# Zero fills, filler products, block means and token buffers in the lead-in of an attention kernel

## The chip, the core and the metric

The kernel runs on one core of a Trainium2 chip. The metric is device time in microseconds (us) of one execution, as the median over runs. The time before the change is 1376.94 us, the median of 3 runs (1375.19 to 1377.54).

## The reference

Three stages follow each other in float32: a sparse attention, a soft mixture of experts over its output, and a two-layer network with a rational activation. Only the attention is touched. It has 2 batches, 8 heads, 768 tokens and head dimension 64. Each query sees the keys less than 16 positions away, and besides them one summary per block of 32 keys: the maximum of the keys, and the mean of the values.

```python
k_sum = k.reshape(B, H, nb, block, D).max(axis=3)
v_sum = v.reshape(B, H, nb, block, D).mean(axis=3)
scores_l = scale * np.matmul(q, k.transpose(0, 1, 3, 2))
mask_l = np.abs(pos[:, None] - pos[None, :]) < window
scores_s = scale * np.einsum('bhsd,bhnd->bhsn', q, k_sum) + np.log(block)
scores_all = np.concatenate([np.where(mask_l, scores_l, -1e9), scores_s], axis=-1)
a = exp(scores_all - max) ; a = a / (sum(a) + 1e-09)
out = np.matmul(a, np.concatenate([v, v_sum], axis=2))
```

Its output, 1536 tokens by 512, is the input of the mixture (8 experts with all tokens in all of them, and a balancing of the gates by rows and columns) and then of the last network.

## The kernel before, in words

Each engine executes its instructions in the order in which the program writes them; a wait on another engine stops all that stands behind it on the same engine. The order is thus the order of the Python code, with one helper: `at(s, f, ...)` puts a function on a list (`todo`) that is worked off near the end of step `s`.

Tokens of k and q are handled in groups of 256 (`LT`), three per batch. A group is loaded by one DMA from the sync engine (`load_nat`, L345) into a buffer of the pool `nat`, copied into token order (`by_token`, L411 and the copy helper L333), transposed on TensorE in two halves of four transposes (`transpose8`, L357) and evacuated from PSUM, by ScalarE in the lead-in (`place`, L366). Which buffer of the pool a new load takes is decided when the program is built; with three buffers the first load of v has to take one that a group of k has occupied.

For the block keys, VectorE takes maxima over the transposed k (`block_keys`, L378, for groups 0 and 1; `last_keys`, L390 and L393, for group 2, straight from PSUM). The evacuation of group 1 is ordered behind the maxima over group 0, because both touch the same tile `kb`.

For the block means of v, GpSimd adds pairs of tokens (`sum_v`, L436), TensorE multiplies with an averaging matrix (`prep_v`, L446, three products of 512 columns that count as six instructions), ScalarE copies the result from PSUM (L453), and GpSimd copies it into the value buffers `vx` of the first three tiles (`block_values`, L333).

Queries are then worked off in 24 tiles of 64 tokens. Step `s` of the main loop (L735) issues, for several tiles at different stages: the scores of tile `s` (`scores`, L517, then the mask addition L524 and the row maximum L528 on VectorE), the outputs of tile `s - 3` (`av`, L567), the transposes of tile `s - 2`'s probabilities (`trans`, L550, evacuated at L552), in the first six steps five filler products on the identity matrix (`spin(5)`, L429), the normalisation of tile `s - 1` on VectorE (`norm`, L541 to L544), the exponentials of tile `s` on ScalarE (`exps`, L537), and the `todo` list of the step. A float32 product on TensorE counts as two MATMUL and two LDWEIGHTS instructions; a transpose counts as one of each.

Ahead of all this stands the setup. GpSimd makes the identity matrix and the masks (`make_mask`, L586 to L594), VectorE spreads the mask over the partitions (L599) and fills `ones`, `wavg`, `am`, the edges of `kb` and `vx` with constants (L611 to L629). `am` are the three probability buffers of the tiles, 128x544 each; `vx` are the three value buffers, 120x512 each.

After the attention, the mixture and the last network run on TensorE for more than 1200 us. Some of their first products and weight loads are mixed into the attention's steps (`main`, `dma_w`).

Of the kernel before, what the change touches and what calls it, by code (L numbers as in the profile page):

```python
# [10 lines left out]
F32 = mybir.dt.float32  # L11
F32R = mybir.dt.float32r
# [10 lines left out]
def kernel(  # L23
# [14 lines left out]
    nc = tc.nc  # L38
    B, H, S, D = q.shape
    NT, DM = out.shape  # L40
    NE, _, FE = w1.shape
    F2 = w_out.shape[0]
    P = 128
# [14 lines left out]
    NB = S // BLK  # L58
    HQ = QT // 2
    VO = 2 * HQ  # L60
    CK = VO + NB
    CO = CK + HQ
# [248 lines left out]
    with ExitStack() as actx:  # L311
        apool = actx.enter_context(tc.tile_pool(name="att", bufs=2, side="right"))
        a1 = actx.enter_context(tc.tile_pool(name="att1", bufs=1, side="right"))
# [3 lines left out]
        am = [a1.tile([P, 2 * AS], F32, name=f"am{i}") for i in range(3)]  # L317
        vx = [a1.tile([CO, DM], F32, name=f"vx{i}") for i in range(3)]
        qs = [a1.tile([P, NP, LT], F32, name=f"qs{i}") for i in range(2)]
        wavg = a1.tile([P, 2 * NB], F32, name="wavg")  # L320
        wavgr = a1.tile([P, 2 * NB], F32R, name="wavgr")
        masks = [a1.tile([P, 4 * HQ + 2 * NB + 2 * (CO - HQ)], F32, name=f"mask{i}") for i in range(3)]

        nat = {}
        kT = {}
# [6 lines left out]
        def pcopy(dst, src):  # L332
            nc.gpsimd.tensor_scalar(out=dst, in0=src, scalar1=1.0, scalar2=0.0, op0=ALU.mult, op1=ALU.add)  # L333

        def load_nat(src, nm, b, i):

            if nm == "q" and b == 0 and i < 2:
                if i:
                    t = spool.tile([P, KC, 2 * P], F32, tag="stg", name="q_0_1")
                else:  # L340
                    t = kb[1].rearrange("p c n -> p (c n)")[:, 0:NP * LT].rearrange("p (c n) -> p c n", c=NP)
                t = t.rearrange("p c (h t d) -> p (c h) t d", h=2, t=2)
            else:
                t = apool.tile([P, H, 2, D], F32, tag="nat", name=f"{nm}_{b}_{i}", bufs=3)
            nc.sync.dma_start(t, src[b, :, i * LT:(i + 1) * LT, :].rearrange("h (p t) d -> p h t d", t=2))  # L345
            nat[nm, b, i] = t

# [71 lines left out]
        def prep_q(b, i):  # L419
            new_q(b, i)  # L420
            for par in range(2):
                place(qT[b, i], par, transpose8("q", b, i, par), qscale, (b, i) == (0, 2))

        def spin(n):

            ps = psm.tile([P, 512], F32, tag="mm", name=f"spin_{len(spins)}")
            spins.append(n)
            for i in range(n):
                nc.tensor.matmul(ps[:, 0:P], lhsT=ident, rhs=ident, start=True, stop=True)  # L429
# [9 lines left out]
        def prep_v(b, *parts):  # L439
            if parts[0] == 0:  # L440
                vps[b] = psm.tile([P, DM], F32, tag="mm", name=f"vps_{b}")
            ps = vps[b]
            nb = LT // BLK
            for i in parts:
                o = (NB - nb) - nb * i
                nc.tensor.matmul(  # L446
                    ps[VO:CK, :], lhsT=wavg[:, o:o + NB],
                    rhs=nat.pop(("vsum", b, i)).rearrange("p h d -> p (h d)"),
                    start=(i == 0), stop=(i == NL - 1), tile_position=(0, VO),
                )  # L450
            if parts[-1] == NL - 1:
                vs[b] = acc[3 + 4 * b]
                (nc.vector.tensor_copy if b else nc.scalar.copy)(vs[b][VO:CK, :], ps[VO:CK, :])  # L453

        def means_split(i):
            x = nat.pop(("vsum", 1, i)).rearrange("p h d -> p (h d)")
            if i < 2:
                y = spool.tile([P, KC, 2 * P], F32R, tag="stg", name=f"vhl_{i}").rearrange("p (a b) f -> p a (b f)", a=2)
            else:
                y = apool.tile([P, 2, DM], F32R, tag="nat", name="vhl_2", bufs=3)  # L460
            nc.scalar.copy(y[:, 0], x)
            nc.gpsimd.tensor_sub(y[:, 1], x, y[:, 0].bitcast(F32))
            means[i] = (y[:, 0], y[:, 1])
# [94 lines left out]
        def av(t):  # L558
            aT = st.pop((t, "aT"))
            if t < 4 and t % 2:  # L560
                ps = psm.tile([P, NP * P], F32, tag="mm", name=f"xo_{t}").rearrange("p (c n) -> p c n", c=NP)
            else:
                ps = psa.tile([P, NP, P], F32, tag="xo", name=f"xo_{t}")
            aT = aT.rearrange("p (s j c q) -> p s j c q", s=2, j=2, c=NP)
            for p in range(NP):
                for j in range(2):
                    nc.tensor.matmul(  # L567
                        ps[j * D:(j + 1) * D, p, 0:QT],
                        lhsT=vx[t % 3][:, (2 * p + j) * D:(2 * p + j + 1) * D],
                        rhs=aT[:, :, j, p, :],  # L570
                        start=True, stop=True,
                    )
            o = t * QT
            dh, dl = xh[:, :, o:o + QT], xl[:, :, o:o + QT]
            nc.scalar.copy(dh, ps[:, :, 0:QT])
            nc.vector.tensor_sub(dl, ps[:, :, 0:QT], dh.bitcast(F32))
# [7 lines left out]
        def make_mask():  # L584
            m = masks[1]
            nc.gpsimd.memset(m, 0.0)  # L586
            nc.gpsimd.memset(m[:, VO:VO + 2 * (HQ + NB)].rearrange("p (s n) -> p s n", s=2)[:, :, 0:NB], math.log(BLK))
            lo = m[:, 0:2 * CK].rearrange("p (s n) -> p s n", s=2)[0:HQ, :, 0:HQ]
            hi = m[:, HQ:HQ + 2 * (CK + NB)].rearrange("p (s n) -> p s n", s=2)[0:HQ, :, 0:HQ]
            nc.gpsimd.affine_select(  # L590
                out=lo, in_=lo, compare_op=ALU.is_ge, fill=NEG, base=-1,
                pattern=[[0, 2], [1, HQ]], channel_multiplier=-1,
            )
            nc.gpsimd.affine_select(  # L594
                out=hi, in_=hi, compare_op=ALU.is_ge, fill=NEG, base=-1,
                pattern=[[0, 2], [-1, HQ]], channel_multiplier=1,
            )
            for p in range(1, NP):
                nc.vector.tensor_copy(m[p * HQ:(p + 1) * HQ, 0:2 * CK], m[0:HQ, 0:2 * CK])  # L599

        def edge_mask(i):
            m = masks[i]
            pcopy(m[:, 0:2 * CK], masks[1][:, 0:2 * CK])
            if i == 0:
                nc.gpsimd.memset(m[:, 0:WIN], NEG)
            else:
                nc.gpsimd.memset(m[:, 2 * CK - WIN:2 * CK], NEG)

        make_mask()
        edge_mask(0)  # L610
        nc.vector.memset(ones, 1.0)  # L611
        nc.vector.memset(wavg, 0.0)
        for m in (wavg[:, NB - LT // BLK:NB],):
# [6 lines left out]
                out=m, in_=m, compare_op=ALU.is_ge, fill=0.0, base=BLK // 2 - 1,  # L620
                pattern=[[BLK // 2, LT // BLK]], channel_multiplier=-1,
            )
        for t_ in am:
            nc.vector.memset(t_, 0.0)
        nc.vector.memset(kb[0][:, :, 0:WIN], 0.0)
        nc.vector.memset(kb[0][:, :, S + WIN:S + 2 * WIN], 0.0)
        nc.scalar.copy(wavgr, wavg)
        for t_ in vx:
            nc.vector.memset(t_, 0.0)  # L629

        def place_k(i, early=False):
            new_k(0, i)
# [36 lines left out]
        def at(s, f, *args):  # L669
            todo.setdefault(s, []).append(lambda: f(*args))  # L670
# [3 lines left out]
        at(9, edge_mask, 2)  # L674
        for o in (0, S + WIN):
            at(2, nc.vector.memset, kb[1][:, :, o:o + WIN], 0.0)
        at(2, block_values, 0)
        at(2, load_nat, k, "k", 1, 1)
        at(2, dma_w, 0, 2, 0, 6)
# [48 lines left out]
        def main(s, us):  # L728
            if mains and mains[0][0] <= s:
                credit[0] += us  # L730
            while mains and mains[0][0] <= s and credit[0] >= mains[0][1] / 2:
                credit[0] -= mains[0][1]
                mains.pop(0)[2]()

        for s in range(NQ + AV):  # L735
            if s < NQ:
                scores(s)
            if s == 2:
                prep_v(0, 0, 1, 2)
            if s == 3:  # L740
                prep_q(0, 1)
            if s >= AV:
                av(s - AV)
                if s - AV + 3 < NQ:
                    load_vx(s - AV + 3)
            main(s, 1.5 if s < 12 else 0.9 if s < 22 else 0)
            if 0 <= s - AV + 1 < NQ:
                trans(s - AV + 1)
                if s < 6:
                    spin(5)  # L750
            if 0 < s <= NQ:
                norm(s - 1)
            if s < NQ:
                exps(s)
                if s == 1:
                    sum_v(0, 2)
                if s == 1:
                    by_token("q", 0, 1)
            for f in todo.pop(s, []):
                f()  # L760
            if s < 22:
                main(s, 0.8 if s < 12 else 0.4)
            elif s < NQ + AV - 1:
                mains.pop(0)[2]()
# [544 lines left out]
```

## Time and profile before

| | |
|---|---|
| median of 3 runs | 1376.94 us (1375.19 to 1377.54) |
| the profiled execution | 1377.25 us, of which the span is 1375.5 us |
| PE (TensorE matmul) busy | 1353.9 us, 98% |
| DVE (VectorE) busy | 1063.6 us, 77% |
| ACT (ScalarE) busy | 516.3 us, 38% |
| POOL (GpSimd) busy | 796.7 us, 58% |
| mean granted TensorE clock | 0.996 of full speed |

The profile is that of one execution, and its times count from the first instruction. PEld is the weight load of TensorE, SP the sync engine, which issues the DMAs. A chain of waits is followed back from the last instruction, at each step to what released it; "issue" in it is time in which the engine waited for nothing that the profile shows. L517 is line 517 of the kernel.

### The profile page before, as it was taken

The page shows a single profiled execution, that of the slowest core. Times are in us where ns is not written, and L with a number is a line of the kernel's source. Part 1 is how long each engine was busy: PE and PEld are TensorE (multiplying, and loading weights), DVE is VectorE, ACT ScalarE, POOL GpSimd, SP SyncE. Part 2 cuts the span into 40 slices and gives each one's busy share as a digit, 9 for nine tenths or more (in the row PEclk, how much of TensorE's full clock was granted, in tenths as well). Part 3 has the DMA queues.
Part 4 walks back from the last instruction along what each step waited for, and adds up shares of the span by engine and source line. Part 5 has one row for each costly group of instructions (what it writes and reads, how often), then busy time and mean ns, then how long its engine had stood idle before and what let it go on. Part 6 is the DMA issues. An engine that isn't in the chain of part 4 may idle for free.

```text
span 1375.5 us, 22596 instructions
## 1 busy us (share of the span) xinstructions
PE 1353.9 (98%) x8547; PEld 1199.1 (87%) x8547; DVE 1063.6 (77%) x1844; ACT 516.3 (38%) x1156; POOL 796.7 (58%) x955
## 2 busy tenths in 40 slices
PE   6999999999999999999999999999999999999998
PEld 4888898899889998899988998899988888888887
DVE  5875578777777877777777777777777689998885
ACT  4676422322222222222222222222222369966662
POOL 3543546777777777677777777677777012222221
PEclk8999999999999999999999999999999999999999
DMA  9541012222222222222222222222221421212102
GB/s 235 140 112 24 16 47 66 67 75 67 82 79 78 76 71 71 67 68 72 75 71 90 74 69 66 76 66 75 68 81 59 139 75 47 77 46 92 31 16 77
DMA packets 119277, 102.55 MB, mean 75 GB/s; under 512 B 30464, under 2 KB 100224, under 8 KB 119168
## 3 DMA queue, kind: packets, MB, share of 16 engines
q1 hardware_dynamic: 119168, 101.10, 24.5%
q8 instruction: 68, 1.11, 0.4%
q14 instruction: 41, 0.34, 0.1%
HBM read 81.15 MB, written 19.92 MB: 73 GB/s over the span
## 4 chain that ended last, share of the span: by engine, by line
PE 95%; DVE 2%; ACT 2%; issue 1%; DMA 0%; POOL 0%; ACTq 0%; POOLq 0%; DVEq 0%
PE p_v L186 12%; PE p_v L187 12%; PE p_v L188 12%; PE p L186 8%; PE p L188 8%; PE p L187 7%; PE X L1092 6%; PE X L1094 6%; PE X L1093 6%; PE Z L1094 3%; PE Z L1093 3%; PE Z L1092 3%; PE Y L1094 2%; PE Y L1093 2%; PE Y L1092 2%; PE sc L517 1%
## 5 line engine op out<-in xcount | busy, mean ns | idle before, releaser
L1204 DVE SCALAR_TENSOR_TENSOR accs<-p_v,Pt,accs 128x512 f32<-128x512 f32 x336 | 244.3, 746 | 90.9 <-PE p_v L188 90.4
L186 PE MATMUL p_v<-w2h_v,hh_v 128*128 128x512 f32 x720 | 282.6, 392 | 0.0
L188 PE MATMUL p_v<-w2h_v,hl_v 128*128 128x512 f32 x720 | 281.7, 391 | 0.0
L187 PE MATMUL p_v<-w2l_v,hh_v 128*128 128x512 f32 x720 | 281.4, 391 | 0.0
L1101 DVE SCALAR_TENSOR_TENSOR hl_v<-s,hh_v 128x384 fp32r<-128x384 f32 x180 | 133.8, 743 | 76.2 <-ACT hh_v L1100 75.0
L236 POOL TENSOR_TENSOR hl<-ta,hh 128x512 fp32r<-128x512 f32 (+1 forms) x52 | 63.1, 1214 | 206.4 <-ACT hh L235 163.5
L1112 ACT COPY s<-X 128x384 f32<-128x384 f32 x56 | 27.1, 484 | 411.2 <-PE X L1094 411.2
L902 POOL TENSOR_SCALAR ce<-ce 128x296 uint32<-128x296 uint32 (+1 forms) x56 | 67.2, 1200 | 181.3 <-DVE ce L893 181.3
L186 PEld LDWEIGHTS p_v<-w2h_v,hh_v 128*128 128x128 f32 x720 | 135.2, 188 | 29.4 <-issue 3.1
L188 PEld LDWEIGHTS p_v<-w2h_v,hl_v 128*128 128x128 f32 x720 | 135.1, 188 | 28.7
L187 PEld LDWEIGHTS p_v<-w2l_v,hh_v 128*128 128x128 f32 x720 | 135.2, 188 | 25.6
L1100 ACT ACTIVATE hh_v<-s 128x384 fp32r<-128x384 f32 x180 | 95.0, 528 | 124.3 <-DVE s L1135 66.7
L112 POOL TENSOR_TENSOR wS<-S,wS 128x256 fp32r<-128x256 f32 x120 | 100.1, 834 | 14.4 <-ACT wS L109 4.7
L186 PE MATMUL p<-xh,w1h 128*128 128x512 f32 (+2 forms) x288 | 103.0, 358 | 0.0
L187 PE MATMUL p<-xl,w1h 128*128 128x512 f32 (+2 forms) x288 | 101.7, 353 | 0.5 <-issue 0.5
L188 PE MATMUL p<-xh,w1l 128*128 128x512 f32 (+2 forms) x288 | 101.8, 353 | 0.0
L186 PE MATMUL p<-w2h,hh 128*128 128x512 f32 (+1 forms) x244 | 95.0, 389 | 0.5 <-DVE accs L264 0.5
L188 PE MATMUL p<-w2h,hl 128*128 128x512 f32 (+1 forms) x244 | 94.5, 387 | 0.2 <-POOL hl L236 0.2
L187 PE MATMUL p<-w2l,hh 128*128 128x512 f32 (+1 forms) x244 | 94.3, 386 | 0.0
L112 POOL TENSOR_TENSOR w2l_v<-sb,w2h_v 128x512 fp32r<-128x512 f32 x60 | 82.8, 1380 | 5.0
L1094 PE MATMUL X<-th,wS 128*128 128x384 f32 x240 | 80.2, 334 | 0.0
L1093 PE MATMUL X<-tl,wS 128*128 128x384 f32 x240 | 80.2, 334 | 0.0
(225 smaller groups left out, 3352.1 us busy)
## 6 DMA issues: line engine op xcount, KB each, us to landing
sa<-in_moe_w_dram SPq DMA_DIRECT2D x30, 512.0 KB, 3.5
sb<-in_moe_w_dram SPq DMA_DIRECT2D x30, 512.0 KB, 4.1
cv<-in_moe_w_in_dram SPq DMA_DIRECT2D x24, 296.0 KB, 2.9
w1h<-f_in SPq DMA_DIRECT2D x16, 256.0 KB, 2.9
w1l<-f_in SPq DMA_DIRECT2D x16, 256.0 KB, 3.3
w2h<-f_out SPq DMA_DIRECT2D x16, 256.0 KB, 4.8
w2l<-f_out SPq DMA_DIRECT2D x16, 256.0 KB, 5.1
f_in<-ch SPq DMA_DIRECT2D x24, 148.0 KB, 4.2
```

The lines of the kernel that those rows point to most:

```text
L112: nc.gpsimd.tensor_sub(lo, src, hi.bitcast(F32))
L186: nc.tensor.matmul(ps, lhsT=sh, rhs=mh, start=(i == 0), stop=False)
L187: nc.tensor.matmul(ps, lhsT=sh, rhs=ml, start=False, stop=False)
L188: nc.tensor.matmul(ps, lhsT=sl, rhs=mh, start=False, stop=(i == n_k - 1))
L236: nc.gpsimd.tensor_sub(hl[:, :n], ta, hh[:, :n].bitcast(F32))
L902: nc.gpsimd.tensor_scalar(out=e, in0=e, scalar1=896, scalar2=0, op0=ALU.subtract, op1=ALU.max)
L1092: nc.tensor.matmul(ps, lhsT=w[:, 0, t], rhs=mh, start=start and t == 0, stop=False, **go)
L1093: nc.tensor.matmul(ps, lhsT=w[:, 0, t], rhs=ml, start=False, stop=False, **go)
L1094: nc.tensor.matmul(ps, lhsT=w[:, 1, t], rhs=mh, start=False, stop=t == 1, **go)
L1100: nc.scalar.activation(hh, src, AF.Relu)
L1101: nc.vector.scalar_tensor_tensor(out=hl, in0=src, scalar=0.0, in1=hh.bitcast(F32), op0=ALU.max, op1=ALU.subtract)
L1204: nc.vector.scalar_tensor_tensor(out=a, in0=ps, scalar=Pt[:, g, e:e + 1], in1=a, op0=ALU.mult, op1=ALU.add)
```

## The change

The `am` fills go to GpSimd and stand behind the rest of the setup. The spreading of the mask becomes a function of its own that VectorE executes behind the `vx` fills, and the copy of the mask for the first tile (`edge_mask(0)`) stands behind it. Ten filler products are issued ahead of the first transposes. The block means of v are no longer issued straight after the scores of step 2 but from that step's `todo` list, which is worked off behind the transposes of tile 0, five filler products and the exponentials of tile 2. The pool of token buffers has four instead of three; two of the three mask tiles are made smaller.

```diff
-        masks = [a1.tile([P, 4 * HQ + 2 * NB + 2 * (CO - HQ)], F32, name=f"mask{i}") for i in range(3)]
+        masks = [a1.tile([P, 4 * HQ + 2 * NB + 2 * (CO - HQ) * (i == 1)], F32, name=f"mask{i}") for i in range(3)]
...
-                t = apool.tile([P, H, 2, D], F32, tag="nat", name=f"{nm}_{b}_{i}", bufs=3)
+                t = apool.tile([P, H, 2, D], F32, tag="nat", name=f"{nm}_{b}_{i}", bufs=4)
...
-                y = apool.tile([P, 2, DM], F32R, tag="nat", name="vhl_2", bufs=3)
+                y = apool.tile([P, 2, DM], F32R, tag="nat", name="vhl_2", bufs=4)
...
+
+        def spread_mask():
+            m = masks[1]
             for p in range(1, NP):
                 nc.vector.tensor_copy(m[p * HQ:(p + 1) * HQ, 0:2 * CK], m[0:HQ, 0:2 * CK])
...
         make_mask()
-        edge_mask(0)
         nc.vector.memset(ones, 1.0)
         nc.vector.memset(wavg, 0.0)
...
-        for t_ in am:
+        spin(10)
+        for t_ in vx:
             nc.vector.memset(t_, 0.0)
         nc.vector.memset(kb[0][:, :, 0:WIN], 0.0)
         nc.vector.memset(kb[0][:, :, S + WIN:S + 2 * WIN], 0.0)
+        spread_mask()
         nc.scalar.copy(wavgr, wavg)
-        for t_ in vx:
-            nc.vector.memset(t_, 0.0)
+        edge_mask(0)
+        for t_ in am:
+            nc.gpsimd.memset(t_, 0.0)
...
+        at(2, prep_v, 0, 0, 1, 2)
         at(2, block_values, 0)
...
             if s < NQ:
                 scores(s)
-            if s == 2:
-                prep_v(0, 0, 1, 2)
             if s == 3:
                 prep_q(0, 1)
```

## Rows read from the trace of the kernel before

**Rows 1.** The page's chain that ended last, share of the span by engine
```profile
PE 95%; DVE 2%; ACT 2%; issue 1%; DMA 0%; POOL 0%; ACTq 0%; POOLq 0%; DVEq 0%
```
**Rows 2.** Chain in order of time up to 16 us: start, length, engine, tile, line
```profile
3.46 0.51 DVE am L624
...
6.41 0.48 DVE vx L629
6.89 0.29 DVE accs L411
...
7.32 1.95 PE kps L357 x8
...
9.29 0.65 ACT kb L366
...
9.96 1.23 DVE ks L378
...
11.28 1.15 ACT kb L366 x2
...
14.90 0.90 DVE ks L393
```
**Rows 3.** The same chain, from 15.8 to 47 us
```profile
15.84 0.64 PE sc L517 x37
...
17.16 1.04 PE sc L517 x41
...
19.80 2.29 issue
...
22.41 5.24 PE vps L446 x6
27.65 0.58 PE at L550 x4
28.23 1.12 PE spin L429 x10
29.35 0.73 PE sc L517 x46
30.08 1.02 PE qps L357 x8
...
46.30 0.45 issue
```
**Rows 4.** Windows: length, busy (count) PE, PEld, DVE, ACT, POOL; PEclk, DMA, GB/s
```profile
17.00:18.00 1.00, 0.84 (x64) 0.84 (x64) 0.62 (x2) 0.31 (x2) 0.67 (x1) 0.63 1.17 290
...
27.00:28.00 1.00, 1.00 (x5) 0.42 (x5) 0.00 (x0) 0.32 (x1) 0.00 (x0) 0.75 1.08 356
```
**Rows 5.** Tile k, first 15 us: its loads (duration ns, first to last start), landing
```profile
L345 SPq DMA_DIRECT2D k<-in_k_dram x3: 432/567/1309, 0.8 to 1.9; - x3
...
DMA to landing us min/median/max: 5.5/6.1/6.7
```
**Rows 6.** Timeline by engine: start, length, operation, shapes [idle before, releaser]
```profile
1.32 0.39 POOL L586 MEMSET mask<- 128x352 f32 x1
...
8.68 1.20 POOL L333 TENSOR_SCALAR accs<-k 128x512 f32<-128x512 f32 x2 [4.33 <-DMA k<-in_k_dram]
10.39 0.62 POOL L333 TENSOR_SCALAR accs<-kb 128x512 f32<-128x512 f32 x1 [0.51 <-DMA kb<-in_q_dram]
...
5.00 0.62 ACT L411 COPY accs<-k 128x512 f32<-128x512 f32 x1
...
20.69 0.53 DVE L544 TENSOR_TENSOR am<-am,sm 128x352 f32<-128x352 f32 x1
```
**Rows 7.** DMA queues, 19 to 20 us: packets, MB, share of 16 engines
```profile
q8 instruction: 1, 0.02, 7.2%
```
**Rows 8.** Sync engine, 9 to 12 us: what it waited for, and its issue
```profile
SPq L345 <- POOL accs L333: 1.3, 1, 1.3
...
9.91 0.37 SPq L345 DMA_DIRECT2D v<-in_v_dram  x1
```

## The prediction

> **What bounds the kernel now.** I read the page's chain of waits first. It lies on TensorE for 95% of the span [rows 1], so the long middle can't gain from this change, whose edits end at about 30 us, and every microsecond won there before TensorE becomes continuously busy should reach the end. So I next read the chain in order of time over the first 48 us, where the reader is to see two stretches that are not matmul work at full speed.
>
> The first runs up to the first scores [rows 2]. VectorE's fills of `am` and `vx` end at 6.89 us; the first copy of k follows them at once; TensorE starts at 7.32; then ScalarE and VectorE alternate (evacuate, reduce, evacuate, reduce) until the block keys are ready and the scores against them start at 15.84. The second [rows 3] is scores of tiles 0 to 2, an "issue" wait of 2.29 us in the middle of tile 2's scores, the block means of v (5.24 us for six products), tile 0's transposes and ten filler products, until tile 3's scores start at 29.35. From there TensorE shows almost no idle time up to 42 us.
>
> Then the windows by microsecond, for the clock [rows 4]: TensorE goes from 2.4 to 1.2 GHz within 17 to 18 us and back within 27 to 28 us, so the block means run at 1.2 GHz.
>
> **Fills to GpSimd, and the order of the rest on VectorE.** The three `am` fills (0.51 us each with 0.06 between, 1.7 in all [rows 2]) leave VectorE, and three mask copies move behind the `vx` fills. VectorE no longer waits for GpSimd's mask before its fills, so it is through them near 3.1 us instead of 6.89. What is late next is the data. The three k transfers are issued from 0.8 to 1.9 us and the known ones land after 5.5 and 6.7 us [rows 5]: the second at about 6.8, the third at 8.6, where GpSimd's wait for it ends [rows 6]. At that spacing of 1.8 us the first lands at 5.0 (estimate); ScalarE's copy of it at 5.00, right behind the preceding instruction, says not later [rows 6]. So the first VectorE copy moves from 6.89 to about 5.05: 1.84 us. On GpSimd the fills cost about 0.6 each by its 128x352 fill (0.39 [rows 6], scaled by columns), 1.8 us between about 3.6 and 5.4; its next work waits for data until 8.68 [rows 6], which hides them. Without that cover they would delay the third k tile by their 1.8 us.
>
> **Ten products ahead of the data.** They are twenty instructions. Ten take 1.12 us at 2.4 GHz [rows 3], so twenty take 2.2 us, or 4.5 us at 1.2 GHz, from about 1.45 (the identity is written before GpSimd's mask fill of 1.32 [rows 6]) to 3.7 or 5.95. TensorE is idle there today. What they buy is the clock for the first transposes: eight of k take 1.95 us from 7.32 [rows 2], eight of q 1.02 us from 30.08 [rows 3]. The windows' column prints 1.00 at 7.32 as well as at 30.08, but the pace is half.
>
> [...] By the printed 1.00 the products would buy nothing, and the first link would gain the 1.84 us alone.
>
> From both sides: if the clock stays at 1.2 GHz until the fillers end at 5.95 and beyond, the eight transposes end at 5.95 + 1.95 = 7.9 instead of 9.27, a gain of 1.4. If it is up by 5.5 (5.05 plus the 0.43 from copy to TensorE), they take about 1.0, and the next limit is the second k tile: landed at 6.8, two copies of 0.36 on VectorE ahead of the reduce there, which then starts at 7.55 instead of 9.96, a gain of 2.4. I take 2.0, since the clock may rise anywhere in between. The links behind keep their lengths (reduce 1.23, two evacuations 1.15, reduces and maximum [rows 2]), and the others are in time: the third k tile is copied by 9.9, and q lands at about 10.35 [rows 6], is copied, transposed and evacuated by about 13. So the scores against block keys start at 13.8 instead of 15.84.
>
> **The wait of 2.29 us, and forty more instructions.** The filler adds 20 products and 20 weight loads ahead of everything. The wait is for no engine; a 16 KB packet of the instruction queue moves in 19 to 20 us [rows 7], and work resumes at 22.09. I read it as TensorE waiting for its next block of instructions. Its end stands 6.25 us behind the start of the block-key scores, in which I suppose the request falls. Forty instructions earlier in the stream the stop comes some 20 products sooner; those are then left over behind it, 0.5 us at the pace of 41 in 1.04 [rows 3]. The request also comes sooner, by nothing up to 0.8 us (the stretch from the q evacuation to the block keys, 13.0 to 13.8). I take 0.5. The two cancel: tile 2's scores end 2.0 us earlier, at 20.4.
>
> [...]
>
> **Block means behind tile 0's transposes.** Six products (5.24), four transposes (0.58) and ten fillers (1.12) [rows 3] change places; TensorE is in order and works off the same 6.94 us. All are in the stretch in which the clock rises, 5.1 us after its start; which of them comes first doesn't change how much is done before and after that. From both sides: a rise some 1.7 us later or earlier costs or gives half of that, 0.85. I take nothing. Tile 2's exponentials no longer stand behind the means' copy on ScalarE; but TensorE had no wait for them, so nothing is won there. What is new: tile 0's outputs need the means through a ScalarE copy and a GpSimd copy, 0.6 each [rows 6] with about 0.25 of signalling, and TensorE covers that with tile 3's scores and the q transposes, 0.73 + 1.02 [rows 3]. That leaves 0.3 of cover; without it the cost would be at most 1.45. Tile 0's normalised rows, which the transposes now ahead of the means wait for, end today at 21.22 [rows 6], and 2.0 earlier at 19.2, in time for 20.4.
>
> **A fourth token buffer.** Today the first v load waits for the third k tile's copies (1.3 us of that at the end) and is issued at 9.91 [rows 8]. With a free buffer it is issued behind q at about 5, and v, q and the weights land some 2 us earlier. No step of the chain up to 31 us waits for them, so I take nothing; the bounds are a loss of 0.2 (q's last packets) and nothing gained.
>
> **Sum.** 2.0 + 0 + 0 = 2.0, and 0.1 for the 0.45 us wait of the same kind at 46.30 [rows 3], which sits elsewhere after the change and may go (ends: all of it gained, or a loss of 0.3). The profiled execution took 1377.25 (span 1375.5 and 1.75 around it); 1375.15 would follow. It lies 0.3 above the median of 1376.94, to which the same 2.1 applies: 1374.8. The forecast's own range, with 1.4 to 2.4 for the first link and 0.85 either way for the clock, is 1373.3 to 1376.2.
>
> **Rivals.** *The block of instructions comes in time.* For it: the stop may fall where the request has long been out. Against: scores eat instructions as fast as before. Then TensorE would be through tile 2's scores by 17.7, and tile 0's normalisation is late next: transposes at 19.2 instead of 22.41, a gain of 3.2, 1373.7. *The clock holds, or is back before the means.* For it: more work ahead of the scores. Against: scores of three tiles and the wait are as thin as today, when the clock fell there. The means would take half of 5.24, a gain of 2.1 + 2.6 = 4.7, 1372.2. *The clock falls early.* TensorE's work between 8 and 13 us now comes in pieces that transfers pace; if the clock falls there, the q transposes (1.0 more) and two tiles' scores (0.4 each) slow down: 2.1 - 1.8 = 0.3, 1376.6. *Slower: the instruction stream becomes the bound.* Between 29 and 46 us TensorE runs short instructions back to back, and the 0.45 at 46.30 shows the stream close to its limit. If the shifted blocks stop it twice more for 2.29, the loss is 4.6 - 2.1 = 2.5, 1379.4; one such stop already eats the gain, and slower than before begins at 2.1 us of new stops. Against it: blocks that TensorE reaches earlier are also requested earlier.
>
> **How the numbers follow.** Forecast 0.50, instructions in time 0.11, clock held 0.12, clock early 0.17, stream-bound 0.10. About 0.2% (2.75 us) is what a measurement here can tell from no change. Above that gain lie some 0.3 of the forecast's chance, most of the first rival's and all of the second's: 0.35. Slower by more than that is under half of the last, with the runs' own spread of 2.35 us added: 0.07. The rest, 0.58, is within. The range 1371.9 to 1377.2 leaves out the stream-bound case and half of the held clock.
>
> **What would show it.** First VectorE copy of k at 5.05; eight first transposes in 1.0 to 1.95 us, ended by 7.9; scores against block keys near 13.8; an "issue" wait of about 2 us inside tile 2's scores, with more products behind it; the means after the fillers; tile 3's scores near 27.3 with no wait of tile 0's outputs behind; v issued near 5. Wrong would be: the first copy still behind fills, the q transposes at half pace, or several new "issue" waits between 27 and 46 us.

## The result and the profile after

The changed kernel takes 1388.04 us (median of 4 runs, 1385.92 to 1389.65) against 1376.70 for the kernel before (median of 4 runs): a ratio of 1.0083 with a 95% interval of 1.0065 to 1.0100. It is 11.3 us slower; the forecast was 1374.8. The profiled execution took 1389.65, with a span of 1387.9 against 1375.5. The page's chain that ended last, share of the span by engine, hardly differs from [rows 1]:

```profile
PE 93%; DVE 2%; ACT 1%; issue 1%; DMA 1%; POOL 1%; SPq 0%; ACTq 0%; DVEq 0%; POOLq 0%
```

The start did what was forecast. The timeline of VectorE, GpSimd and TensorE in the first 14 us of the changed kernel (start, length, engine, line, operation, tiles, count, idle before and its end):

```profile
5.06 0.45 DVE L411 COPY accs<-k 128x512 f32<-128x512 f32 x1 [1.40 <-DMA k<-in_k_dram]
...
4.19 1.81 POOL L634 MEMSET am<- 128x544 f32 x3
...
1.42 4.39 PE L429 MATMUL spin<-ident 128*128 128x128 f32 x20 [1.42 <-POOL ident masks.py:199]
5.65 1.04 PE L357 MATMUL kps<-ident,accs 128*128 128x128 f32 x8
...
13.08 0.35 PE L517 MATMUL sc<-kb,qs 64*32 64x64 f32 x16 [0.33 <-ACT qs L366]
13.21 0.27 PE L517 MATMUL sc<-ks,qs 64*32 64x24 f32 x16
```

The copy of k starts at 5.06 instead of 6.89, the first transposes end at 6.7 instead of 9.27 [rows 2]. The scores against the keys of the tokens (`kb`) start at 13.08, those against the block keys (`ks`) at 13.21 instead of 15.84. The chain of waits from 16.9 to 29 us (start, length, what):

```profile
16.91 3.25 issue
...
20.70 1.04 PE at L550 x4
21.74 2.13 PE spin L429 x10
23.87 3.71 PE vps L446 x6
...
28.32 1.02 PE qps L357 x8
```

It answers to [rows 3]: the q transposes that stood at 30.08 now stand at 28.32, 1.76 us earlier, although the wait in front has grown from 2.29 to 3.25. Up to here the change is a gain.

The loss comes later. In the table of TensorE's waits in the first 150 us (line, waited for, total, times, longest), the kernel before has for "issue" only the two waits of [rows 3], 2.29 in scores and 0.45 in a product of the next stage. The changed kernel has:

```profile
PE xo L567 <- issue: 8.1, 3, 3.7
PE sc L517 <- issue: 3.2, 1, 3.2
```

The 8.1 us are new: three waits inside the output products of a tile (`xo`), at which no engine is waited for. The chain of the changed kernel shows where each lies and what follows:

```profile
43.12 1.10 issue
...
51.01 3.35 issue
54.36 0.48 PE xo L567 x3
...
55.36 0.21 PE p L187
...
94.52 0.65 PE xo L567 x15
95.17 3.66 issue
98.83 0.27 PE xo L567
...
99.82 0.43 PE p L187
```

The products `p` of the next stage behind the second and the third wait take 0.21 and 0.43 us each. In the chain of the kernel before, the first-layer products take 0.12 each, and the second-layer ones 0.23:

```profile
52.50 0.12 PE p L187
...
90.65 0.43 PE p L186
91.08 0.23 PE p L187
```

The windows of the changed kernel tell why (length, busy share and count of PE, PEld, DVE, ACT, POOL; then the granted clock, DMA share, GB/s):

```profile
53.00:54.00 1.00, 0.00 (x0) 0.00 (x0) 0.00 (x0) 0.00 (x0) 0.40 (x1) 0.60 0.03 8
54.00:55.00 1.00, 0.64 (x4) 0.52 (x4) 0.00 (x0) 0.12 (x1) 0.00 (x0) 0.50 0.00 0
...
60.00:61.00 1.00, 1.00 (x69) 0.78 (x67) 0.64 (x1) 1.00 (x5) 0.00 (x0) 0.98 0.23 28
...
98.00:99.00 1.00, 0.17 (x1) 0.00 (x0) 0.00 (x0) 0.00 (x0) 1.00 (x2) 0.50 0.08 14
104.00:105.00 1.00, 1.00 (x18) 0.62 (x24) 0.00 (x0) 0.45 (x1) 0.00 (x0) 0.80 0.00 0
```

TensorE stood idle from 51.01 and from 95.17 us, the granted clock fell from 1.00 to 0.50 while it was idle (the window from 53 us prints 0.60, that from 98 us 0.50), and the twelve products behind each wait were run at 0.50 before it rose again near 60 and 104 us (0.98 and 0.80 in the windows from there).

The account goes by the starts of the output products of each tile in both traces. Tiles 0 to 4 stand 1.8 us earlier than before. The wait of 1.10 in tile 4 takes the place of the one of 0.45 at 46.30 [rows 3], 0.7 lost. Between the starts of tile 5's and tile 6's outputs 5.7 us are lost: the wait of 3.35, and 2.4 by which the work behind it takes longer at the granted clock of 0.50. At tile 14's it is 6.25: 3.66, and 2.5 at 0.50 (twelve products in 5.4 instead of 3.0 us). -1.8 + 0.7 + 5.7 + 6.25 = +10.85 at tile 15, which holds through tile 23. Most of the rest of the 12.4 us between the two spans comes near 711 and 717 us, in this one execution; the medians differ by 11.3.

**Why there.** Count the instructions between two such waits. Windows of the changed kernel:

```profile
20.15:43.12 22.97, 22.56 (x504) 17.68 (x504) 12.90 (x33) 13.09 (x50) 8.90 (x15) 0.87 0.82 219
44.22:51.01 6.79, 6.41 (x126) 5.88 (x126) 6.14 (x13) 4.29 (x15) 3.07 (x4) 1.00 0.90 238
92.04:95.17 3.13, 2.98 (x127) 2.53 (x126) 2.88 (x9) 3.13 (x16) 0.00 (x0) 1.00 0.77 225
54.36:95.17 40.81, 39.84 (x884) 34.14 (x884) 29.50 (x68) 27.47 (x104) 16.88 (x19) 0.93 0.39 95
```

PE and PEld together: 1008, 252, and 1768 between waits, that is about 4, 1 and 7 times 252. With TensorE's semaphore instructions, which are in the trace but not in these two columns, it is exactly 256 each: the four waits of the changed kernel fall at TensorE's instructions 449, 1473, 1729 and 3521, which are 4, 1 and 7 times 256 apart, the two of the kernel before at 449 and 1473. So every wait stands at the end of a block of 256 TensorE instructions, the 16 KB that one packet of the instruction queue brings. The page counts as many packets as the 17397 matmuls, weight loads and semaphore instructions make blocks:

```profile
q8 instruction: 68, 1.11, 0.3%
```

In the kernel before the blocks have the same length (its window from 46.75 to 87.68 us has 885 + 884, again seven), but end forty instructions further on in the work: the wait of 0.45 stands 13 output products and 7 products `p`, two instructions each, behind the place at which the changed kernel waits 1.10. Two of its blocks:

```profile
46.75:54.08 7.33, 6.95 (x125) 6.49 (x125) 6.32 (x14) 4.14 (x15) 4.98 (x6) 1.00 0.70 186
87.68:94.10 6.42, 6.37 (x126) 5.19 (x126) 5.11 (x13) 4.24 (x20) 1.93 (x3) 1.00 0.91 230
```

The block from 87.68 holds scores and outputs up to those of tile 14 and the twelve second-layer products behind them, 6.42 us of work, and there is no wait at its end. In the changed kernel the corresponding block (from 92.04) ends one product short of the outputs' end. The twelve long products have fallen into the next block; 253 short instructions are through in 3.13 us, and TensorE waits 3.66: 6.79 us from one end to the next. The packet for the block that follows moves within 91 to 92 us before and within 96 to 97 after, in both about 4 us behind the preceding end. At all four waits of the changed kernel TensorE goes on 2.7 us after the packet has started (at 17.44, 41.50, 51.64 and 96.13). So, as an estimate from these two times, a block whose work takes much less than some 6.5 us is waited for if the packet for the next comes that late; the one of 6.42 before was just in time. Short work alone does not make a wait: the block from 88.00 to 92.04 of the changed kernel took 4.04 us and no wait follows it, since its packet had moved within 89 to 90 us. By count most ends of blocks show no such wait: 4 of the 68 blocks have one, 8.1 + 3.2 = 11.3 us in all.

### The profile page after: what moved, and what is told of

Same layout as the page of the kernel before. It is cut to its first block, busy times and chain, and to the rows that moved or that the text cites. A ratio compares the mean times of both kernels' runs of the same rounds, so it can differ in the third digit from the quotient of the medians.

```text
span 1387.9 us, 22639 instructions
## 1 busy us (share of the span) xinstructions
PE 1362.6 (98%) x8567; PEld 1206.6 (87%) x8567; DVE 1059.6 (76%) x1841; ACT 514.7 (37%) x1156; POOL 797.8 (57%) x958
## 4 chain that ended last, share of the span: by engine, by line
PE 93%; DVE 2%; ACT 1%; issue 1%; DMA 1%; POOL 1%; SPq 0%; ACTq 0%; DVEq 0%; POOLq 0%
PE p_v L186 12%; PE p_v L187 12%; PE p_v L188 12%; PE p L186 8%; PE p L188 7%; PE p L187 7%; PE X L1096 6%; PE X L1098 6%; PE X L1097 6%; PE Z L1098 3%; PE Z L1097 3%; PE Z L1096 3%; PE Y L1098 2%; PE Y L1097 2%; PE Y L1096 2%
```

## The experiments

Theory A says: the forty instructions of the ten leading products shift every later block end; some then stand ahead of long products instead of behind them, TensorE runs dry there, and the clock falls on top. Rivals were the four buffers with their earlier loads, the moved block means, and GpSimd's fills.

**Take the filler out of the changed kernel.**

```diff
-        spin(10)
+        pass
```

> The changed kernel without the ten filler products ahead of the data, all else as changed. Theory A (the forty instructions of the filler move the ends of TensorE's instruction blocks to places where the next block is not there yet): the waits at 51 and 95 us go, the lead-in still gains some 1.3 us of VectorE's shorter queue, so about 1375.5. Theory B (the fourth token buffer lets two loads follow each other at 46 us, and the packet of instructions waits behind them): the wait near 51 us stays with its slow clock, the one near 95 us too, since its loads are the same: 1386 or more. If the first needs both and the second only the filler: 1375.5 as by A, and only the other three kernels tell A from it.

1375.85 us (1374.58 to 1377.08, 10 runs), ratio to before 0.9996 [0.9987, 1.0006]: the whole loss is gone. The waits in `xo` are gone too; TensorE's waits:

```profile
PE sc L517 <- issue: 3.9, 2, 3.0
...
PE kps L357 <- issue: 0.6, 1, 0.6
```

**Three token buffers in the changed kernel.**

```diff
-                t = apool.tile([P, H, 2, D], F32, tag="nat", name=f"{nm}_{b}_{i}", bufs=4)
+                t = apool.tile([P, H, 2, D], F32, tag="nat", name=f"{nm}_{b}_{i}", bufs=3)
...
```

> The changed kernel with three token buffers as before, filler kept. Theory A: both waits stay, about 1388. Theory B: the wait near 51 us goes with the 5.7 us that stand there between the output products of tiles 5 and 6, the one near 95 us stays: about 1382.

1382.88 (1380.13 to 1384.40, 4 runs), 1.0043 [1.0028, 1.0058]. About half the loss stays: theory A's 1388 is missed, and theory B's 1382 is met. Its chain has the same three waits (the first 0.41). The one in tile 14's outputs stays, as theory A says, and the one in tile 5's is shorter, with full pace behind it, as theory B says:

```profile
50.12 1.17 issue
...
51.94 0.12 PE p L187
...
90.08 4.49 issue
...
95.56 0.43 PE p L187
```

**The filler alone in the kernel before**, nothing else of the change.

```diff
+        spin(10)
         for t_ in am:
             nc.vector.memset(t_, 0.0)
```

> The kernel before with the ten filler products alone, VectorE's queue and the three buffers as before. Theory A: new waits for instructions near 52 and 97 us, some 12 us, less 0.5 for the faster first transposes: about 1388. Theory B: no wait near 52, at most the one near 97: 1376 to 1382.

1384.31 (1379.61 to 1384.65, 4 runs), 1.0048 [1.0030, 1.0065]: less than theory A's 1388 and more than theory B's 1376 to 1382. The ten products do harm by themselves, with the same wait in tile 14, but in tile 5 it is only 0.87 with three buffers:

```profile
53.19 0.87 issue
...
92.87 3.66 issue
...
97.53 0.43 PE p L187
```

**Four buffers alone in the kernel before** (with the smaller mask tiles that make room).

```diff
...
-                t = apool.tile([P, H, 2, D], F32, tag="nat", name=f"{nm}_{b}_{i}", bufs=3)
+                t = apool.tile([P, H, 2, D], F32, tag="nat", name=f"{nm}_{b}_{i}", bufs=4)
...
```

> The kernel before with the fourth token buffer alone (and the two smaller masks that make room for it). Theory A: no new wait, 1376.7 as before. Theory B: a wait for instructions near 53 us and the clock falling behind it, 1382.

1377.03 (1375.38 to 1377.84, 10 runs), 1.0002 [0.9992, 1.0011]: nothing. So the fourth buffer costs only where the shifted blocks are: 1388.04 with both, 1384.31 and 1377.03 with either. Theory A as first put, that the shift makes the whole loss whatever the buffers, is too strong: the shift is needed, and the earlier loads make it dearer.

**Keep the ten leading products and take as many filler products away in steps 4 and 5**, which puts all later block ends back.

```diff
-                if s < 6:
+                if s < 4:
                     spin(5)
```

> The changed kernel, with the ten filler products ahead of the data but without the five fillers of step 4 and the five of step 5, so that behind step 5 TensorE's instructions stand where they stood before the change. Theory A (where the ends of the 256-instruction blocks fall): no wait near 95 us, and none of 3 us near 51, where the block's end falls behind the twelve first-layer products again; about 1375, and 2.2 us less own filler time where that is on the path. If the filler at the front does the harm in another way (the clock, a PSUM buffer, the start of TensorE), the wait near 95 us stays: 1385 or more.

1374.30 (1373.78 to 1375.82, 10 runs), 0.9988 [0.9978, 0.9997]. This is the sharpest test: the whole change is in, the leading filler too, and only the count of instructions ahead of step 6 is as before. Of the 13.7 us between this and the changed kernel some 1.5 are the products taken out (in its trace the outputs of tile 1 stand 1.27 us earlier than before, those of tile 3 2.74); the other 12 go with the position of the block ends. TensorE's waits for instructions are again only at scores (3.5 us in two) and transposes (0.85).

**Ten products in step 8 instead of at the start.**

```diff
-        spin(10)
+        pass
...
+                if s == 8:
+                    spin(10)
```

> The changed kernel without filler ahead of the data, but with ten filler products in step 8, at some 63 us. Theory A: the block whose end falls among tile 14's output products gets the wait of some 3.6 us again, with the slow clock behind it, and nothing new at 51 us: 1375.9 of the kernel without filler, 1.1 for the products themselves and 5 to 7 for the wait and the clock, 1382 to 1384. If the harm comes from the front: 1377.

1383.76 (1380.21 to 1385.84, 4 runs), 1.0053 [1.0035, 1.0071]: the harm needs no filler in the lead-in. Its products themselves take 2.4 us there; the wait in tile 14's outputs is back with 3.7.

**About the same time of filler in fewer instructions**: three products of 512 columns in all of 12 instructions, instead of ten of 128 columns in 40. `wide` is a new function that issues them.

```diff
...
-        spin(10)
+        wide(3)
```

> The changed kernel with three filler products of 512 columns instead of ten of 128: 1536 columns against 1280, but 12 TensorE instructions instead of 40. Theory A: the end of the block that fell among tile 14's output products now falls behind the twelve second-layer products (12 instructions further on than before the change, of 15 that are there), so no wait at 95 us; near 51 us it falls on the last of the twelve first-layer products, so at most 1 us: about 1375.5. If busy time of the filler does the harm: 1388.

1377.28 (1375.72 to 1379.28, 10 runs), 1.0009 [0.9999, 1.0019]. The two long waits are gone (the longest behind 30 us is the 0.94 of its chain at 43.81), and the 1388 of a filler whose busy time does the harm is refuted. But it is no gain either and lies 1.8 above theory A's 1375.5, with several waits of 0.3 to 0.9.

**Issue two loads of v one step later and one of weights two steps later in the changed kernel.**

```diff
-            at(6 + i, load_nat, v, "v", 1, i)
+            at((6, 8, 9)[i], load_nat, v, "v", 1, i)
...
-        at(15, dma_sub, 0, 2)
+        at(17, dma_sub, 0, 2)
```

> The changed kernel with the filler and four buffers, but the second and third v load of batch 1 one step later each, and the first expert's second weight load two steps later, so that at 46 and at 91 us one load stands where two stood back to back. Theory that the packet of instructions waits behind the loads that were issued ahead of it: near 51 us the packet comes 2 us earlier and the wait shrinks from 3.35 to about 1, near 95 us from 3.66 to about 2, and with less idle time the clock stays up: 1377 to 1380. If the packet's delay doesn't depend on the loads: 1388 as the changed kernel.

1381.48 (1378.36 to 1383.72, 5 runs), 1.0039 [1.0025, 1.0053]: 6.6 us better than the changed kernel, but still 5.3 slower than before and 1.5 above the range that was expected. The sync engine's issues in the changed kernel ahead of the wait at 51.01:

```profile
46.19 0.40 SPq L345 DMA_DIRECT2D q<-in_q_dram  x1
46.69 0.53 SPq L345 DMA_DIRECT2D v<-in_v_dram  x1
```

Two loads of 512 KB stand back to back, and the packet moves only within 51 to 52 us, over 7 us after TensorE went on with the preceding block at 44.22. Before, the v load came at 50.46, and the packet for this block end moved within 50 to 51 us, 3.9 after TensorE went on at 46.75. With the v load taken from there, the waits become:

```profile
50.00 1.98 issue
...
52.97 0.21 PE p L187
...
92.46 1.76 issue
...
94.86 0.23 PE p L187
```

1.98 for 3.35 and 1.76 for 3.66, and the second-layer products at 0.23, as in the kernel before. Loads ahead of a packet explain part of its lateness; 1.98 us remain with the loads apart, and what holds the packet then was not settled.

**Both remedies, and the other two parts alone.** Without the leading products and with the loads apart:

> The changed kernel without the ten leading products, and with two loads issued later. Theory A (the shifted ends of instruction blocks cost the time): without the forty instructions the ends are where they were before, so this stands with the run without the filler, 1375.9, and later loads, which shorten only waits that lie in long products, add at most 0.3: 1375.3 to 1376.2. Rival (the loads that stand close together cost time by themselves, filler or not): the 5 to 7 us that later loads gave back with the filler come again in part, 1373 or less.

1374.93 (1373.69 to 1376.14, 11 runs), 0.9991 [0.9982, 1.0000]. The ten leading products, ten fewer in steps 4 and 5, and the loads apart:

> The changed kernel with ten leading products, ten filler products fewer in steps 4 and 5, and two loads issued later. Theory A: the fewer fillers alone gave 1374.3, with the long waits gone; what is left of waits for instructions behind the first is 0.85 and 0.32 us, and later loads can take away at most these: 1373.3 to 1374.5. Rival (later loads are worth 6.6 us whatever the block ends): about 1368.

1374.91 (1373.31 to 1376.07, 11 runs), 0.9990 [0.9981, 0.9999]. The first lies 0.4 below theory A's range, the second 0.4 above it, and neither near the rivals' 1373 and 1368: loads that stand apart are worth at most 1 us where no long wait is left to shorten.

The block means alone, in the kernel before:

```diff
-            if s == 2:
-                prep_v(0, 0, 1, 2)
...
+        at(2, prep_v, 0, 0, 1, 2)
         at(2, block_values, 0)
```

> The kernel before with only the block means of v moved behind the transposes and fillers of tile 0. Prediction's step: nothing, with 0.85 us of gain or loss at the ends: 1375.5 to 1377.2 beside 1376.4 for before. Theory A adds: no instruction is added, all block ends behind the move stay, so nothing else changes. Rival: the move changes where the clock rises or makes tile 0's outputs wait for the means, over 1 us slower, above 1377.4.

1376.54 (1375.29 to 1379.43, 12 runs), 1.0003 [0.9995, 1.0012]: nothing, as the prediction took it.

The fills alone (the probability buffers on GpSimd, the mask's spreading behind the `vx` fills), three buffers, no leading products:

```diff
-        for t_ in am:
+        for t_ in vx:
             nc.vector.memset(t_, 0.0)
...
+        spread_mask()
...
+        edge_mask(0)
+        for t_ in am:
+            nc.gpsimd.memset(t_, 0.0)
```

> The kernel before with only the fills: the probability buffers on GpSimd, the mask's spreading behind the value buffers' fills; no leading products, three token buffers, block means where they were. Prediction's step: the first copy of k moves from 6.89 to about 5.05, and with the transposes at half pace the lead-in gains 1.4 to 1.84 us: 1374.6 to 1375.0. Theory A: no TensorE instruction is added, so all of that gain reaches the end. Rival (what the lead-in wins is lost again at the next wait for instructions, since blocks are asked for no earlier): 1376.0 or more.

1374.10 (1373.21 to 1374.92, 11 runs), 0.9985 [0.9976, 0.9993], the fastest median here and faster than both kernels; the versions around 1374.3 to 1374.9 can't be told from it. 2.0 us are gained, where 1.4 to 1.84 were expected, and the end keeps them. Its timeline:

```profile
4.94 0.57 DVE L411 COPY accs<-k 128x512 f32<-128x512 f32 x1 [1.28 <-DMA k<-in_k_dram]
...
12.97 0.35 PE L517 MATMUL sc<-kb,qs 64*32 64x64 f32 x16 [0.35 <-ACT qs L366]
...
13.94 0.27 PE L517 MATMUL sc<-ks,qs 64*32 64x24 f32 x13 [0.63 <-DVE ks L393]
```

Of waits for instructions only those in the scores are left, 3.1 us in two. Without any leading product tile 0's scores start at 12.97, with them at 13.08. Those against the block keys start at 13.94 here and at 13.21 in the changed kernel, but with the same leading products at 14.07 in the run with fewer fillers and at 14.20 in the one with three buffers.

## Why the prediction was wrong

**Fills to GpSimd: right.** First copy at 5.06 (forecast 5.05), fills hidden on GpSimd (1.81 us, 4.19 to 6.0; forecast 1.8), and alone they are worth 2.0 us of median (forecast 1.84).

**Ten products, the lead-in: half right.** The transposes end by 6.7, within the forecast's cases, and the reduce of VectorE behind them starts at 7.54 (forecast 7.55). The eight transposes take 1.04 us behind the ten products, 1.95 before [rows 2] and 1.96 in the run without the filler; the windows print a granted clock of 1.00 beside all three, so that in the lead-in the pace alone shows the gain. The prediction's 1.2 GHz answers to the pace of the second-layer products at a granted clock of 0.50 in the changed kernel, 512 columns every 0.427 us or 1.2 columns per ns; its 2.4 answers to twice that, an estimate from the products of the block means there, 0.854 us apart at 0.50 and 0.43 at 1.00. The scores against block keys start at 13.21 (forecast 13.8), 2.6 earlier than before, where 1.4 to 2.4 were allowed. That the filler won this isn't shown: with it they start at 13.21, 14.07 and 14.20 in three traces, without it at 13.94 and 14.16 in two. The 13.21 owes much to the maximum L393, which took 0.19 us there and 0.64 to 1.24 in the other four; the last section says why, and the forecast left its 0.90 as it was.

**"The wait of 2.29 us, and forty more instructions": the step that failed.** The prediction saw the wait at a block of instructions, saw that forty instructions more bring its end forward, and worked this out for that one block: "The two cancel", with 0.1 to gain for the wait at 46.30. It did not do the same for the other block ends, though each moves by the same forty. That term was sized between 0.3 lost and 0.45 won. Measured, the shifted ends, with the loads where the change puts them, cost 0.7 + 5.7 + 6.25 = 12.65 us in the profiles, and about 12 us of median by the run in which the ends are moved back. Even the one block was misjudged: the packet came within 17 to 18 us instead of 19 to 20 [rows 7], some 2 us earlier, but TensorE reached the end 2.9 us earlier, so that the wait grew by 0.96; the products left over behind it took 0.55, as estimated.

**The rival "the instruction stream becomes the bound"** named the mechanism and had a chance of 0.10. Its price, two more stops of 2.29, was too low twice: the two long stops took 3.35 and 3.66, and the clock fell in each, for another 2.4 and 2.5, which it left out. It looked for them between 29 and 46 us, where only the one of 1.10 fell. Its sentence against, that blocks reached earlier are also asked for earlier, does not hold in tile 14's block: its end is reached earlier because the long products have left it, and its packet still moves about 4 us behind the preceding end.

**A fourth buffer "I take nothing": right alone, wrong in company.** Alone it is 1.0002. With the filler it lets a v load go out 0.5 us behind a q load, and the wait in tile 5's outputs is 3.35 instead of 1.17. The prediction looked for engines that wait for the loads, not for the instruction packet among them. Why a packet is late without such loads (1.98 us of wait remain with the loads apart) stays open.

**Block means moved: right.** They are 1.0003 alone. In the changed kernel transposes, fillers and means together take 1.04 + 2.13 + 3.71 = 6.88 us against the 6.94 of before: the transposes and fillers run at the granted clock of 0.50 (all windows from 21 to 24 us) in place of half of the means. No wait for tile 0's outputs shows in the chain up to 30 us.

**Two sums of the prediction** are slightly off, and nothing hangs on them. Its own range, from 1.4 to 2.4, 0.85 either way and the 0.1, comes out as 1373.6 to 1376.3, not 1373.3 to 1376.2. In the first rival tile 2's scores would end at 18.1 (22.41 less 2.29 and 2.0), not 17.7.

## What to carry to other kernels

Where TensorE works off many short instructions, adding or removing any of them ahead moves all later ends of 256-instruction blocks (forty instructions here moved them by twenty products); read the "issue" waits at those ends, and see what work stands in each block between two of them. A block with long products in it gives the next packet time to come (6.42 us of work here); one of 253 short instructions (3.13 us) did not when that packet started 4 us late. Before filler is added, try the same change with the count of instructions kept, and keep large loads from being issued close together just ahead of such a block (3.35 us of wait behind two loads 0.5 us apart here, 1.98 with them apart).

## What the runs showed of the hardware

A wait for instructions of 3.35 us cost more than itself: the granted clock fell from 1.00 to 0.50 inside it, and the work behind it lost another 2.4 us. Of the waits of 0.87 to 1.98 us in the output products (the filler alone, three buffers, the loads apart), only the one of 1.98 was followed by half pace, with first-layer products at 0.21.

A small operation on VectorE took longer beside an addition on GpSimd that works on other tiles, 0.90 us against 0.19. The maximum L393 over 128x32 took 0.90 us before [rows 2] and ended at 15.79, beside GpSimd's addition of v (14.44 to 15.74). In the changed kernel it falls ahead of that addition and takes 0.19:

```profile
12.48 0.19 DVE L393 TENSOR_TENSOR ks<-ks,odd 128x32 f32<-128x32 f32 x1
...
12.70 1.31 POOL L436 TENSOR_TENSOR accs<-v 128x512 f32<-128x512 f32 x1 [1.55 <-DMA v<-in_v_dram]
```

In the run with fewer fillers it falls into the addition and ends 0.05 us behind it:

```profile
12.90 1.12 DVE L393 TENSOR_TENSOR ks<-ks,odd 128x32 f32<-128x32 f32 x1
...
12.67 1.30 POOL L436 TENSOR_TENSOR accs<-v 128x512 f32<-128x512 f32 x1 [1.46 <-DMA v<-in_v_dram]
```

The traces of all 14 kernels here agree: the maximum takes 0.19 us in the two in which it does not overlap the addition (the changed kernel, four buffers alone), and 0.60 to 1.24 in the twelve in which it does, where it ends within 0.1 us behind the addition.
